# A two-branch transformer block on one core: where three tiles are transposed, who issues three small loads, and the order of two kinds of DMA transposes

## The chip, the cores and the metric

The kernel runs on one core of one Trainium2 chip. The time of a run is the device time in microseconds (us) of that core, from one launch; the figures below are medians of several runs. The engines named are TensorE (PE; its weight loads are PEld), VectorE (DVE), ScalarE (ACT), GpSimd (POOL) and SyncE (SP). SyncE computes nothing here: it issues DMAs, and ScalarE issues a few more.

## The reference

Input x has 2048 rows of 448 values in bf16. With xn = layernorm(x), the result is x + A(xn) + B(xn).

```python
# A: linear attention with 16 heads of 28
qkv = xn @ wqkv                                   # q, k, v
pq, pk = q @ w_phi[h], k @ w_phi[h]               # per head
phi_q = [softmax(pq), softmax(-pq)]               # the same for phi_k
kv, z = phi_k^T v, sum(phi_k)
A = (phi_q kv / (phi_q z + 1e-6)) @ wo
# B: on xn, with a normalization of its own
h  = gelu(layernorm(xn) @ w1)                     # (2048, 448)
x1 = xn + shift(h) @ w2                           # four column groups moved by 1, -1, 2, -2 rows
B  = x1 + gelu(layernorm(x1) @ w3) @ w4           # 448 -> 1792 -> 448
```

## The kernel before, in words

The 2048 rows are 16 tiles of 128. A small class, Recorder, takes every operation in the order in which the program states it (`op`, and its helpers `mm`, `tr`, `act`, `ew`, `dma`, `dma_t`), works out from the bytes that each reads and writes which semaphore waits are needed (`solve`, line 75), and then plays each engine's operations in that order. So each engine, and each queue of DMAs, runs strictly in program order; the order in the text is the schedule. In the profile all matmuls have line 188 (`mm`), PE transposes 192 (`tr`), ScalarE's operations 196 (`act`), those of VectorE and POOL 200 (`ew`), DMA transposes 203 (`dma_t`) and other DMAs 206 (`dma`).

**Loads (lines 339 to 358).** SyncE and ScalarE issue the tiles of x, wv and w1. Then SyncE issues, in this order: the transposes of the weights of k (`load_wT(1, c)`, four DMA transposes into hi), w2, the four loads of phi's blocks into bd (the line after 353, after POOL has zeroed bd), and two of the four transposes of q's weights (`load_wT(0, c)`). ScalarE's table of gelu is loaded by `table` (line 374).

**Normalization.** `ln1_stats` (line 430) takes VectorE's statistics of a tile (`bn_stats`, `bn_aggr`) and lets POOL work out the scale (`ln1_scale`: an addition and a power of -1/2); `ln1_apply` (448) writes the normed tile xn, on VectorE or POOL; `ln1_again` works out the scale of the second normalization for four tiles at a time.

**Transposing xn.** Every product of xn needs xnT, the tile with its columns on the partitions. `xn_T(i, b)` (line 467) does it with four PE transposes into bank b and one eviction by ScalarE. `xn_Td(i)` (473) does it with one DMA transpose from SyncE. Tiles 0 to 11 take the first way, 12 to 15 the second.

**Octets.** `octet(g)` (line 710) computes V = xn wv and the input of h (xn w1) of the four tiles of group g. It handles two tiles after the other in full-height matmuls of V and of w1 (`full`), then the half-height remainders of those two (`tail`, two at a time), then the half-height parts of the next two tiles, whose full parts follow. So the first use of an octet's third and fourth tile is in the half-height matmuls. `v_pair` evicts V by ScalarE or VectorE (`evac` names who does the third and fourth tile), `w_pair` evicts through gelu on ScalarE into h_tok. PE transposes of later tiles are put between the matmuls of an octet.

**What follows the octets.** `h_T(i)` (line 554) transposes tile i of h by DMA, SyncE again; `w2_mul(i)` (598) multiplies tile i with w2 and needs h of tiles i - 1, i and i + 1 because of the shifts. `fold(t, m, b, eng)` (457) multiplies a block of wT with phi's blocks bd, giving the weights of pq and pk at once. After octet 3 ScalarE issues w3 (`load_rest`, line 796). Then come the softmax inputs of k and q, with `w2_tile(4, 6)` (825) early among them, and `kv_tile`.

**The plan (from line 876).** Nine stages, each with two or three groups of w3 matmuls and a list of steps, written out by hand. N is `num_tile` (the attention's numerator and denominator of a tile: PE, a chain on VectorE, a product on POOL into o_tok), O is `o_T` (the DMA transpose of that tile of o into oT), E is `eq_T` (two DMA transposes of a tile of phi_q into eqT, one of four slots, which N of the tile four later reads), Ff is `fin_full` (the product with w4 and wo, which reads oT), St the store of a tile. SyncE issues E, O, St and the transposes of the second normalization's output in the order in which the list has them.

Of the kernel before, what the change touches and what calls it, by code (L numbers as in the profile page):

```python
# [5 lines left out]
ACT = mybir.ActivationFunctionType  # L6
# [202 lines left out]
def bass_parallel_sum__linear_kernel_hedgehog__mixer_s_mlp__prompt_kernel(  # L209
# [3 lines left out]
    H, DH = A_w_phi.shape[0], A_w_phi.shape[1]  # L213
# [3 lines left out]
    CR = 112  # L217
# [7 lines left out]
    with es:  # L225
        R = Recorder(nc, es)
# [13 lines left out]
        def new(name, cols, dt=BF16):  # L240
            return view(region(name, cols * DTB[dt]), cols, dt)
# [9 lines left out]
        xtok = new("xtok", NT * D).rearrange("p (t d) -> p t d", t=NT)  # L251
# [18 lines left out]
        bd = new("bd", 512).rearrange("p (c h e) -> p c h e", c=NC, h=4)  # L270
# [17 lines left out]
        st = new("st", NT * 8, F32).rearrange("p (t c) -> p t c", t=NT)  # L288
        mv = new("mv", NT * 8, F32).rearrange("p (t c) -> p t c", t=NT)
# [28 lines left out]
        def tview(b, n=512, base=0):  # L318
            return b[:, :].bitcast(BF16)[:, base:base + n]

        dve, pool = "DVE", "POOL"
# [28 lines left out]
        for c in range(NC):  # L350
            load_wT(1, c)
        R.dma(w2[0:CR, :, :], B_w2.rearrange("(m p) d -> p m d", p=CR))
        R.ew("POOL", "memset", bd[0:CR, :, :, :], 0.0)
        for k in range(4):
            p = slice(DH * k, DH * k + DH)
            R.dma(bd[p, :, k, 0:DH], A_w_phi[k::4].rearrange("c e f -> e c f"))
        for c in range(2):
            load_wT(0, c)

# [21 lines left out]
        R.ew(pool, "memset", epss[:, :, 1], LN_EPS * LN_EPS / (1.0 + LN_EPS))  # L381
        R.ew(pool, "memset", hT[:, :, 0:PAD], 0.0)
        R.ew(pool, "memset", hT[:, :, S + PAD:HW], 0.0)
        busy = gT[:, 0, 0, 0:256]
        R.ew(dve, "memset", busy, 1.0)
        R.ew(dve, "memset", vp[:, :, DH + 1:HP], 0.0)
# [22 lines left out]
        def lap(a):  # L409
            return bass.AP(a.tensor, a.offset, [list(a.ap[0]), [192, 2], [1, 256]])  # L410

        def halves(a):
            return a.rearrange("p (b e) -> p b e", b=2)

        def ln_stats(stt, mvt, src, i):
            R.ew(dve, "bn_stats", stt[:, i, 0:6], src[:, i, 0:D])
            R.ew(dve, "bn_aggr", mvt[:, i, 0:2], stt[:, i, 0:6])
# [8 lines left out]
        def ln_apply(eng, dst, src, mvt, rst, i, k=0):  # L426
            m, op = (mvt[:, i, 0:1], ALU.subtract) if eng == dve else (rst[:, i, 1:2], ALU.add)
            R.ew(eng, "tensor_scalar", dst, src, m, rst[:, i, k:k + 1], op0=op, op1=ALU.mult)

        def ln1_stats(a, n, neg):  # L430
            for i in range(a, a + n):
                ln_stats(st, mv, xtok, i)
            ln1_scale(a, n, neg)

        def ln1_scale(a, n, neg):
            R.ew(pool, "tensor_tensor", mv[:, a:a + n, 2:4], mv[:, a:a + n, 1:2].to_broadcast([128, n, 2]), epss[:, 0:n, :],
                 op=ALU.add)
            R.ew(pool, "tensor_tensor", rs[:, a:a + n, 2:4], mv[:, a:a + n, 2:4], mhalf2[:, 0:n, :], op=ALU.pow)
            if neg:
                R.ew(pool, "tensor_scalar", rs[:, a:a + neg, 1], mv[:, a:a + neg, 0], -1.0, 0.0, op0=ALU.mult,  # L440
                     op1=ALU.add)

        def ln1_again(a, n):
            R.ew(dve, "scalar_tensor_tensor", rs[:, a:a + n, 0], rs[:, a:a + n, 3], (1.0 + LN_EPS) ** -0.5,
                 mv[:, a:a + n, 2], op0=ALU.mult, op1=ALU.mult)
            R.ew(dve, "tensor_tensor", rs[:, a:a + n, 4], rs[:, a:a + n, 0], rs[:, a:a + n, 2], op=ALU.mult)

        def ln1_apply(eng, i):
            ln_apply(eng, halves(xn[:, i, :]), lap(xtok[:, i, :]), mv, rs, i, 2)
# [3 lines left out]
        def spin(n, cols):  # L453
            for _ in range(n):
                R.mm(banks[3][:, 0:cols], busy[:, 0:128], busy[:, 0:cols], True, True)
# [11 lines left out]
        def xn_T(i, b):  # L467
            b = banks[b]
            for kc in range(KC):
                R.tr(tview(b)[:, 128 * kc:128 * kc + 128], xn[:, i, 128 * kc:128 * kc + 128], ident[:, :])  # L470
            R.act(xnT[:, :, 128 * i:128 * i + 128], tview(b).rearrange("p (c d) -> p c d", c=KC), ACT.Copy)

        def xn_Td(i):
            R.dma_t(xnT[:, :, 128 * i:128 * i + 128], xn[:, i, :])

        def full(o, first):
            out, lhs, rhs, k = o
            for kc in (0, 3, 2 - k):
                R.mm(out, lhs(kc, 0, 128), rhs(kc, 0, 128), first and kc == 0, not first and kc == 2 - k)
# [14 lines left out]
        def v_pair(i, b):  # L494
            def out(eng="ACT"):
                vd = vaug[:, i:i + 2, :].rearrange("p t (h e) -> p t h e", e=HP)[:, :, :, 0:DH]
                vs = two(b)[:, :, 0:D].rearrange("p t (h e) -> p t h e", e=DH)
                if eng == "ACT":
                    R.act(vd, vs, ACT.Copy)
                else:  # L500
                    R.ew(eng, "tensor_copy", vd, vs)
            return [tok(wv, i, b), tok(wv, i + 1, b + 1)], out
# [51 lines left out]
        def h_T(i):  # L554
            R.dma_t(hT[:, :, PAD + 128 * i:PAD + 128 * i + 128], h_tok[i])
# [139 lines left out]
        def ln1_two(i):  # L695
            ln_stats(st, mv, xtok, i)
            ln1_apply(dve, i - 1)
            ln_stats(st, mv, xtok, i + 1)
            ln1_scale(i, 2, 1)
            ln1_apply(pool, i)  # L700

        def ln1_some(a, n):
            for i in range(a, a + n):
                ln1_stats(i, 1, 0)
                if i:
                    ln1_apply(dve, i - 1)
                if i == 4:
                    ln1_again(0, 4)

        def octet(g, evac="ACT", first="ACT", late=None):  # L710
            i = 4 * g
            v, w = v_pair(i, 0), w_pair(i, 2)
            v2, w2 = v_pair(i + 2, 4), w_pair(i + 2, 6)
            if g == 0:
                spin(19, 256)
                xn_T(0, 4)
                spin(5, 128)
                xn_T(1, 5)
                full(v[0][0], True)
                full(v[0][1], True)  # L720
                xn_T(2, 6)
                full(w[0][0], True)
                xn_T(3, 7)
                full(w[0][1], True)
            else:
                full(v[0][0], True)
                full(w[0][0], True)
                if i + 2 < 12:
                    xn_T(i + 2, 4)
                    xn_T(i + 3, 5)  # L730
                full(v[0][1], True)
                full(w[0][1], True)
            for p in (v, w):
                for o in p[0]:
                    tail(o, False)
            for p in (v2, w2):
                for o in p[0]:
                    tail(o, True)
            v[1](first)
            w[1]((0,))  # L740
            for o in v2[0]:
                full(o, False)
            if i + 4 < 12:
                xn_T(i + 4, 0)
                xn_T(i + 5, 1)
            if late:
                late()
            w[1]((1,))
            v2[1](evac)
            for o in w2[0]:  # L750
                full(o, False)
            w2[1]()

        ln1_some(0, 8)
        ln_stats(st, mv, xtok, 8)
        ln1_apply(dve, 7)
        octet(0, "DVE")
        ln_stats(st, mv, xtok, 9)
        ln1_scale(8, 2, 1)
        ln1_apply(pool, 8)  # L760
        ln1_again(4, 4)
        ln1_two(10)
        for i in range(4):
            h_T(i)
        octet(1, "DVE")
        ln1_apply(dve, 11)
        ln1_again(8, 4)
        ln1_stats(12, 2, 0)
        ln1_stats(14, 2, 0)
        for i in range(12, 16):  # L770
            ln1_apply(dve, i)
        h_T(4)
        for i in range(12, 16):
            xn_Td(i)
        for c in range(2, NC):
            load_wT(0, c)
        for i in range(5, 8):
# [71 lines left out]
        N, O, E, St, Ff = num_tile, o_T, eq_T, store, fin_full  # L849
# [23 lines left out]
        def stats2(i):  # L873
# [7 lines left out]
                      ]),  # L881
            (0, 2, 4, 6, [(N, 1, 0), (E, 5), (O, 1), (Ff, 0), (W, 11, 3), (sc, 2), (N, 2, 0), (E, 6), (O, 2), (N, 3, 6), (E, 7), (O, 3),
                          (Ff, 1)]),
            (0, 2, 6, [(Ff, 2), (St, 0), (ga, 2), (W, 12, 2), (N, 4, 0), (E, 8), (O, 4), (N, 5, 6), (E, 9), (O, 5), (W, 13, 3), (Ff, 3),
                       (St, 1),]),
            (0, 2, 6, [(Ff, 4), (St, 2), (W, 14, 2), (W, 15, 3), (sc, 3), (N, 6, 0), (E, 10), (O, 6), (N, 7, 6), (E, 11), (O, 7),
                       (Ff, 5), (St, 3), (ga, 3)]),
            (0, 2, 6, [(Ff, 6), (St, 4), (N, 8, 0), (E, 12), (O, 8), (N, 9, 6), (E, 13), (O, 9), (Ff, 7), (St, 5),]),
            (0, 2, 6, [(Ff, 8), (St, 6), (N, 10, 0), (E, 14), (O, 10), (N, 11, 6), (E, 15), (O, 11), (Ff, 9), (St, 7)]),
            (0, 2, 6, [(Ff, 10), (St, 8), (N, 12, 0), (O, 12), (N, 13, 6), (O, 13), (Ff, 11), (St, 9)]),  # L890
            (0, 2, 6, [(N, 14, 0), (O, 14), (Ff, 12), (St, 10), (N, 15, 2), (O, 15), (Ff, 13), (St, 11)])]
# [53 lines left out]
```

## Time and profile before

| | us |
|---|---|
| median of 3 runs | 181.6 |
| lowest and highest | 181.51, 182.17 |
| the profiled execution | 181.43 |
| its span, first to last instruction | 179.7 |

The profile is of one execution. Its times are microseconds from the start of the span. A row of the timeline has start, duration, engine, line, operation, tiles written and read, shape and how many were merged; in brackets stands how long the engine was idle before and what ended that. Names of buffers are without their numbers: xnT is also the memory of o and oT, vaug of the attention's scratch, hi of the first tiles of h and of the transposed weights. A q behind an engine's name (SPq, ACTq) marks an issue of a DMA; "to landing" is the time from issue to the arrival of the last byte's signal.

### The profile page before, as it was taken

What the parts mean: (1) busy time and instruction counts of PE and PEld (TensorE: products, weight loads), DVE (VectorE), ACT (ScalarE), POOL (GpSimd) and SP (SyncE); (2) the same over time, 40 slices, a digit from 0 to 9 for tenths busy, and PEclk for the clock granted to TensorE, in tenths of its full rate; (3) what the DMA queues carried; (4) which work ended last, traced back from release to release, by engine and by line L of the source; (5) the groups of instructions that cost most, each with busy time, mean ns of one, the idle gap of its engine ahead of it and who ended that gap; (6) DMA issues with size and microseconds to landing.
All of it is one profiled execution on the core that took longest, in us unless ns stands there. A gap on an engine that the chain in (4) does not pass through costs nothing.

```text
span 179.7 us, 3181 instructions
## 1 busy us (share of the span) xinstructions
PE 175.9 (98%) x1218; PEld 90.5 (50%) x1218; DVE 117.6 (65%) x269; ACT 80.2 (45%) x99; POOL 94.6 (53%) x144
## 2 busy tenths in 40 slices
PE   7999999999999999999999999999999999999994
PEld 5554655454445444654554654553554544635564
DVE  5898679659999999584594296196282352655531
ACT  2378881798999639777105104103206006014000
POOL 7774582067999797002457526037835063151660
PEclk9999999999999999999999999999999999999999
DMA  5998555499465498473245545432554654120231
GB/s 166 338 218 134 102 87 104 89 341 223 89 90 106 98 277 172 91 160 60 58 88 89 89 101 104 110 62 58 113 112 99 82 138 96 43 59 28 55 106 51
DMA packets 59142, 21.04 MB, mean 117 GB/s; under 512 B 50744, under 2 KB 58616, under 8 KB 59128
## 3 DMA queue, kind: packets, MB, share of 16 engines
q1 hardware_dynamic: 55656, 16.56, 45.8%
q10 hardware_dynamic: 3472, 4.29, 8.0%
q8 instruction: 9, 0.15, 0.3%
q14 instruction: 5, 0.04, 0.1%
HBM read 7.08 MB, written 1.84 MB: 50 GB/s over the span
## 4 chain that ended last, share of the span: by engine, by line
PE 95%; DVE 3%; ACT 0%; issue 0%
PE bank L188 93%; PE bank L192 2%; DVE vaug L200 1%; DVE st L200 1%; DVE xn L200 1%; ACT xnT L196 0%; DVE mv L200 0%; DVE gT L200 0%
## 5 line engine op out<-in xcount | busy, mean ns | idle before, releaser
L196 ACT ACTIVATE phik<-bank 128x1024 bf16<-128x1024 f32 (+1 forms) x44 | 40.2, 991 | 68.1 <-PE bank L188 67.9
L188 PE MATMUL bank<-gT,w 128*128 128x512 bf16 (+1 forms) x224 | 46.1, 380 | 0.1
L188 PE MATMUL bank<-w,phik 128*128 128x448 bf16 (+2 forms) x238 | 45.2, 342 | 0.0
L200 DVE TENSOR_TENSOR vaug<-bank,vaug 128x464 f32<-128x464 f32 (+3 forms) x65 | 33.1, 514 | 17.4 <-PE bank L188 12.3
L200 POOL TENSOR_TENSOR xnT<-vaug 128x196 bf16<-128x196 f32 (+1 forms) x32 | 18.0, 585 | 49.2 <-DVE vaug L200 49.2
L188 PEld LDWEIGHTS bank<-w,phik 128*128 128x128 bf16 x238 | 22.6, 98 | 18.4 <-issue 0.2
L188 PEld LDWEIGHTS bank<-gT,w 128*128 128x128 bf16 (+1 forms) x224 | 17.9, 97 | 24.0 <-issue 5.1
L200 POOL TENSOR_TENSOR phik<-phik,rks 128x896 bf16<-128x896 bf16 x15 | 25.8, 1754 | 1.0 <-DVE rks L200 0.9
L200 POOL TENSOR_TENSOR vaug<-xn,xtok 128x448 f32<-128x448 bf16 x16 | 16.3, 1029 | 1.4 <-DVE vaug L200 1.4
L200 DVE TENSOR_TENSOR xn<-bank,xn 128x448 bf16<-128x448 f32 x16 | 9.4, 597 | 11.5 <-PE bank L188 11.5
L200 DVE TENSOR_REDUCE ksum<-phik 128x32 f32<-128x896 bf16 x16 | 16.6, 1035 | 0.0
L200 DVE RECIPROCAL vaug<-bank 128x16 f32<-128x16 f32 x16 | 3.6, 228 | 17.9 <-PE bank L188 17.9
L188 PE MATMUL bank<-wo,xnT 128*128 128x448 bf16 (+3 forms) x68 | 14.7, 344 | 0.0
L200 POOL TENSOR_TENSOR rs<-mv,mhalf 128x2 f32<-128x2 f32 (+1 forms) x16 | 13.8, 863 | 1.3
L188 PE MATMUL bank<-w,hT 112*128 112x448 bf16 x64 | 14.2, 352 | 0.0
L188 PE MATMUL bank<-wv,xnT 128*128 128x448 bf16 (+1 forms) x64 | 14.0, 354 | 0.1
L188 PE MATMUL bank<-w,xnT 128*128 128x448 bf16 (+1 forms) x64 | 13.9, 352 | 0.0
L188 PE MATMUL bank<-wpk,xnT 128*128 128x448 bf16 (+1 forms) x64 | 12.2, 354 | 0.0
L188 PE MATMUL bank<-wpq,xnT 128*128 128x448 bf16 (+1 forms) x64 | 12.1, 354 | 0.0
L196 ACT ACTIVATE eq<-bank 128x896 bf16<-128x896 f32 x12 | 10.0, 923 | 1.4 <-PE bank L188 1.4
L200 POOL TENSOR_SCALAR mv<-mv 128x4 f32<-128x4 f32 x4 | 0.8, 203 | 18.2 <-DVE mv L200 18.2
L200 DVE BATCH_NORM_STATS2 st<-xtok 128x6 f32<-128x448 bf16 x16 | 9.8, 612 | 0.8 <-DMA xtok<-in_A_x_dram 0.7
(66 smaller groups left out, 179.2 us busy)
## 6 DMA issues: line engine op xcount, KB each, us to landing
w<-in_B_w_dram ACTq DMA_DIRECT2D x2, 896.0 KB, 6.4
out_dram<-vaug SPq DMA_DIRECT2D x15, 112.0 KB, 1.9
w<-in_B_w_dram ACTq DMA_DIRECT2D x1, 1568.0 KB, 8.7
xtok<-in_A_x_dram SPq DMA_DIRECT2D x2, 448.0 KB, 6.8
wo<-in_A_wo_dram SPq DMA_DIRECT2D x2, 224.0 KB, 2.8
w<-in_B_w_dram SPq DMA_DIRECT2D x1, 392.0 KB, 4.4
hi<-eq SPq DMA_TRANSPOSE x24, 2.5
xtok<-in_A_x_dram SPq DMA_DIRECT2D x3, 112.0 KB, 3.0
```

The source lines that it names most:

```text
L188: self.op("PE", lambda e: e.matmul(out, lhsT, rhs, start=start, stop=stop, skip_group_check=True), [out], [lhsT, rhs])
L192: self.op("PE", lambda e: e.transpose(out, in_, ident), [out], [in_, ident])
L196: self.op("ACT", lambda e: e.activation(out, in_, func, **kw), [out], [in_] + aps)
L200: self.op(eng, lambda e: getattr(e, name)(out, *args, **kw), [out], aps)
```

## The change

There are five edits.

1. Loads: zeroing bd and the four loads of phi's blocks move behind the zeroing of hT's edges, and so behind all the loads above on SyncE; three of the four are issued by ScalarE, behind its table load, one by SyncE.
2. Normalization: the statistics of tiles 8 to 13 are taken one tile at a time instead of in pairs (`ln1_two` is no longer used), and VectorE applies all of them; POOL applied tiles 8 and 10.
3. Transposing xn: PE does tiles 0 to 8; tiles 9, 10 and 11 go to SyncE as DMA transposes. Tiles 9 and 10 stand behind h_T(0) and h_T(1), tile 11 behind them, then h_T(2) and h_T(3); h_T(4) moves from ahead of tiles 12 to 15 to behind them.
4. V of tiles 6 and 7 is evicted by ScalarE (octet 1 without "DVE"; tiles 4 and 5 were ScalarE's before).
5. Plan: in the stages with N 4 and 5 and with N 8 and 9, O comes ahead of E.

```diff
@@ loads
-        R.ew("POOL", "memset", bd[0:CR, :, :, :], 0.0)
-        for k in range(4):
-            p = slice(DH * k, DH * k + DH)
-            R.dma(bd[p, :, k, 0:DH], A_w_phi[k::4].rearrange("c e f -> e c f"))
         for c in range(2):
             load_wT(0, c)
...
         R.ew(pool, "memset", hT[:, :, S + PAD:HW], 0.0)
+        R.ew("POOL", "memset", bd[0:CR, :, :, :], 0.0)
+        for k in range(4):
+            p = slice(DH * k, DH * k + DH)
+            R.dma(bd[p, :, k, 0:DH], A_w_phi[k::4].rearrange("c e f -> e c f"), "ACT" if k else "SP")
@@ octet
-                if i + 2 < 12:
-                    xn_T(i + 2, 4)
-                    xn_T(i + 3, 5)
+                if g == 1:
+                    xn_T(6, 4)
+                    xn_T(7, 5)
...
-            if i + 4 < 12:
-                xn_T(i + 4, 0)
-                xn_T(i + 5, 1)
+            for k in range(2 - g):
+                xn_T(i + 4 + k, k)
@@ octets and what stands between them
-        ln1_some(0, 8)
-        ln_stats(st, mv, xtok, 8)
-        ln1_apply(dve, 7)
+        ln1_some(0, 9)
         octet(0, "DVE")
-        ln_stats(st, mv, xtok, 9)
-        ln1_scale(8, 2, 1)
-        ln1_apply(pool, 8)
+        ln1_stats(9, 1, 0)
+        ln1_apply(dve, 8)
         ln1_again(4, 4)
-        ln1_two(10)
-        for i in range(4):
+        for i in range(10, 12):
+            ln1_stats(i, 1, 0)
+            ln1_apply(dve, i - 1)
+        for i in range(2):
             h_T(i)
-        octet(1, "DVE")
+        for i in range(9, 11):
+            xn_Td(i)
+        octet(1)
+        ln1_stats(12, 1, 0)
         ln1_apply(dve, 11)
+        xn_Td(11)
+        for i in range(2, 4):
+            h_T(i)
         ln1_again(8, 4)
-        ln1_stats(12, 2, 0)
+        ln1_stats(13, 1, 0)
+        ln1_apply(dve, 12)
         ln1_stats(14, 2, 0)
-        for i in range(12, 16):
+        for i in range(13, 16):
             ln1_apply(dve, i)
-        h_T(4)
         for i in range(12, 16):
             xn_Td(i)
+        h_T(4)
         for c in range(2, NC):
             load_wT(0, c)
@@ plan, two stages
-            ... (N, 4, 0), (E, 8), (O, 4), (N, 5, 6), (E, 9), (O, 5), ...
+            ... (N, 4, 0), (O, 4), (E, 8), (N, 5, 6), (O, 5), (E, 9), ...
-            ... (N, 8, 0), (E, 12), (O, 8), (N, 9, 6), (E, 13), (O, 9), ...
+            ... (N, 8, 0), (O, 8), (E, 12), (N, 9, 6), (O, 9), (E, 13), ...
```

More of the change, by code (lines that the diff above doesn't have):

```diff
@@ L883, in bass_parallel_sum__linear_kernel_hedgehog__mixer_s_mlp__prompt_kernel @@
                           (Ff, 1)]),
-            (0, 2, 6, [(Ff, 2), (St, 0), (ga, 2), (W, 12, 2), (N, 4, 0), (E, 8), (O, 4), (N, 5, 6), (E, 9), (O, 5), (W, 13, 3), (Ff, 3),
+            (0, 2, 6, [(Ff, 2), (St, 0), (ga, 2), (W, 12, 2), (N, 4, 0), (O, 4), (E, 8), (N, 5, 6), (O, 5), (E, 9), (W, 13, 3), (Ff, 3),
                        (St, 1),]),
@@ L887, in bass_parallel_sum__linear_kernel_hedgehog__mixer_s_mlp__prompt_kernel @@
                        (Ff, 5), (St, 3), (ga, 3)]),
-            (0, 2, 6, [(Ff, 6), (St, 4), (N, 8, 0), (E, 12), (O, 8), (N, 9, 6), (E, 13), (O, 9), (Ff, 7), (St, 5),]),
+            (0, 2, 6, [(Ff, 6), (St, 4), (N, 8, 0), (O, 8), (E, 12), (N, 9, 6), (O, 9), (E, 13), (Ff, 7), (St, 5),]),
             (0, 2, 6, [(Ff, 8), (St, 6), (N, 10, 0), (E, 14), (O, 10), (N, 11, 6), (E, 15), (O, 11), (Ff, 9), (St, 7)]),
```

## The prediction

> **What bounds the kernel now.** First I read busy time per engine and the chain that ended last, both on the page:
>
> ```profile
> PE 175.9 (98%) x1218; PEld 90.5 (50%) x1218; DVE 117.6 (65%) x269; ACT 80.2 (45%) x99; POOL 94.6 (53%) x144
> PE 95%; DVE 3%; ACT 0%; issue 0%
> ```
>
> TensorE holds 98% of the span and 95% of the chain. Matmul ends are modelled, so I then read starts in the timeline of PE through octets 1 and 2, where the change works:
>
> ```profile
> 18.46 0.61 PE L192 MATMUL bank<-ident,xn 128*128 128x128 bf16 x8
> 18.91 1.30 PE L188 MATMUL bank<-w,xnT 128*128 128x448 bf16 x6
> 20.05 0.73 PE L188 MATMUL bank<-wv,xnT 128*128 128x448 bf16 x3
> 21.18 0.61 PE L192 MATMUL bank<-ident,xn 128*128 128x128 bf16 x8
> 23.25 0.35 PE L188 MATMUL bank<-wv,xnT 64*128 64x448 bf16 x2
> ```
>
> Six 448-column matmuls start at 18.91 and the next group starts at 20.05: 0.19 us each, without a hole. So PE is fed here, and the kernel gains only by giving PE less to do, or by removing one of its few waits; a new wait of PE's is paid in full. The eight transposes at 18.46 (tiles 8 and 9) and at 21.18 (tiles 10 and 11) are what the change thins out; the row at 23.25 is the half-height matmuls of V for tiles 10 and 11, the first use of those two tiles.
>
> The second resource is SyncE's queue, which issues every DMA transpose in program order. Its timeline:
>
> ```profile
> 12.39 1.78 SPq L206 DMA_DIRECT2D bd<-in_A_w_phi_dram  x4
> 14.22 2.43 SPq L203 DMA_TRANSPOSE hi<-in_A_wqkv_dram  x2
> 16.69 1.74 SPq L203 DMA_TRANSPOSE hT<-hi  x1
> 18.48 1.26 SPq L203 DMA_TRANSPOSE hT<-hi  x1
> 19.79 1.27 SPq L203 DMA_TRANSPOSE hT<-hi  x1
> ```
>
> The rows follow each other without a hole: this queue is full here, one transpose each 1.31 us (18.48 to 19.79), the first of hT stretched to 1.79 (16.69 to 18.48). How long after its issue a transpose lands is told by tile hT between 16 and 26:
>
> ```profile
> DMA to landing us min/median/max: 2.5/2.5/3.0
> ```
>
> **The change part by part.**
>
> *Twelve transposes leave PE.* Eight take 18.91 - 18.46 = 0.45 us, so 0.056 each; tiles 9, 10 and 11 are twelve: **-0.68 us**, all of it on the chain. ScalarE loses their three evictions, which is worth nothing by itself.
>
> *Three DMA transposes join SyncE's queue, and three phi loads leave it.* The four loads hold the queue from 12.39 to 14.22, 0.46 each; with three gone, and wT's transposes ahead of the fourth, h_T(0) issues at 16.69 - 1.37 = 15.32. Behind it stand h_T(1), tile 9, tile 10, tile 11. One of the first two will be stretched as h_T(0) is now (1.79), the others take 1.31: tile 9 issues at 18.42, tile 10 at 19.73, tile 11 at 21.04. Are they normed by then? VectorE and POOL say so:
>
> ```profile
> 13.63 1.08 DVE L200 CAST vaug<-bank 128x896 bf16<-128x896 f32 x1
> 14.63 0.61 DVE L200 BATCH_NORM_STATS2 st<-xtok 128x6 f32<-128x448 bf16 x1
> 15.28 0.18 DVE L200 BATCH_NORM_AGGREGATE mv<-st 128x2 f32<-128x6 f32 x1
> 16.86 0.41 DVE L200 TENSOR_SCALAR xn<-xtok,mv,rs 128x512 bf16<-128x512 bf16 x1 [0.36 <-POOL rs L200]
> 12.57 0.69 POOL L200 TENSOR_TENSOR rs<-mv,mhalf 128x2 f32<-128x2 f32 x1
> ```
>
> Statistics cost 14.63 to 15.46 = 0.83, the apply 0.41, and POOL's square root 0.69 runs beside the next tile's statistics. After the cast, with 0.4 for ln1_again, tile 9 is normed at about 17.5, tile 10 at 18.7, tile 11 at 20.0: about 1 us ahead of the queue each time. VectorE keeps that pace because the cast of V of tiles 6 and 7, as long as the one at 13.63, moves to ScalarE, which gives up three evictions of tiles for it; banks 4 and 5, which that V leaves free, are wanted again only at 22.5. So the queue decides, not the engines.
>
> Landing 2.5 later: tile 9 at 20.92, tile 10 at 22.23, tile 11 at 23.54. PE, with its transposes gone, wants tile 9 at 21.18 - 0.23 = 20.95 (just met), and tiles 10 and 11 at 23.25 - 0.68 = 22.57. Tile 10 is there; **tile 11 is 0.97 late**, with 0.05 to start about **+1.0 us** of PE wait. No view shows this wait before, so I bound it: without the stretch 0.5; with the slowest landing of the row (3.0) 1.5. It can't be below zero, since PE waits or doesn't. I take 1.0, the median landing.
>
> At this place a page speaks against the stretch: the Trainium skill (Runtime: NRT & Kernel Launch, Instruction fetch mechanics) holds that refilling an engine's instructions is one queue bump, mostly hidden. This case has such a refill beside the stretched issue, by the DMA view from 16.3 to 16.6:
>
> ```profile
> q8 instruction: 1, 0.02, 19.8%
> ```
>
> By the page the stretch would be no part of the sum, and the wait 0.5 in place of 1.0; by the row the refill sits in the very slice where the queue slows, so the trace leans the other way without proving it.
>
> *What else is moved past SyncE.* h_T(2), h_T(3) and h_T(4) go behind the new ones. h_T(3) lands near 26.2, h_T(4) (now after tiles 12 to 15) near 33; their readers on PE are later by a microsecond or more. Tile 15 would issue at 21.04 + 6 x 1.31 = 28.9, land at 31.4, and is wanted by the row below at 31.82 - 0.68 + 1.0 = 32.1:
>
> ```profile
> 31.82 0.35 PE L188 MATMUL bank<-wv,xnT 64*128 64x448 bf16 x2
> ```
>
> All of this costs nothing in the forecast. From there the queue runs about 2 us later than now, which is the first rival below.
>
> *Three phi loads on ScalarE* stand between its table load and its first eviction:
>
> ```profile
> 3.27 1.28 ACT L372 ACT_TABLE_LOAD   x1 [3.27 <-issue]
> 6.10 0.60 ACT L196 ACTIVATE xnT<-bank 128x512 bf16<-128x512 bf16 x1 [1.55 <-PE bank L192]
> 7.07 0.60 ACT L196 ACTIVATE xnT<-bank 128x512 bf16<-128x512 bf16 x1 [0.37 <-PE bank L192]
> 2.75 0.49 ACTq L206 DMA_DIRECT2D xtok<-in_A_x_dram  x1
> 3.18 2.08 SPq L206 DMA_DIRECT2D xtok<-in_A_x_dram  x3
> ```
>
> 3 x 0.46 from 4.55 ends at 5.93, inside the 1.55 of idle; another 0.37 of slack lies ahead of the second eviction. Cost 0.
>
> *o ahead of q* matters where PE waits for o. In the stage that treats tiles 8 and 9:
>
> ```profile
> 132.10 1.13 POOL L200 TENSOR_TENSOR xnT<-vaug 128x196 bf16<-128x196 f32 x2 [2.59 <-DVE vaug L200]
> 133.97 2.50 SPq L203 DMA_TRANSPOSE hi<-eq  x2
> 136.52 1.26 SPq L203 DMA_TRANSPOSE xnT<-xnT  x1
> xnT<-xnT SPq DMA_TRANSPOSE x1, 4.3
> 125.86 2.81 PE L188 MATMUL bank<-w,phik 128*128 128x448 bf16 x14
> 128.51 0.73 PE L188 MATMUL bank<-wo,xnT 128*128 128x448 bf16 x3
> 138.07 2.81 PE L188 MATMUL bank<-w,phik 128*128 128x448 bf16 x14
> 140.84 0.36 PE L188 MATMUL bank<-wo,xnT 128*128 128x448 bf16 x1
> ```
>
> o of tile 8 is ready at 133.23, yet issues at 136.52 behind q's two transposes and lands 4.3 later, at 140.8; wo's product starts 2.77 after its group's start where the stage before needed 2.65. With o first it issues at 133.97 and lands 2.5 to 4.3 later, by 138.3 at worst: **-0.12 us**. q, then 1.3 later, is read a stage on. In the other stage nobody waits for o: 0.
>
> **Sum:** -0.68 + 1.0 - 0.12 = +0.20 us, against the profiled execution's 181.43 (span 179.7 and 1.7 around it): 181.6. The median of the runs shown is 181.60, 0.17 above that execution, so on its scale 181.8. With the wait at 0.5 and 1.5, and o worth 0 at the upper end, 181.3 to 182.4.
>
> **The rivals.**
>
> *The transposes are in time* (181.60 - 0.80 = 180.8). SyncE would have to reach tile 11 a microsecond sooner. For it: PE's transposes are surely gone and the queue is 1.37 earlier. Against it: a step of 1.31 in every undisturbed pair of rows. A plain store is quicker:
>
> ```profile
> 161.20 0.58 SPq L206 DMA_DIRECT2D out_dram<-vaug  x1
> ```
>
> With steps near that 0.58, tile 11 would be bounded by its norm at 20.0, land at 22.5, and no wait would be left. The Trainium skill says as much (Advanced Engine Details and Errata, X-Bar Transpose (TRN2)): transpose DMAs are as fast as regular ones. The trace doesn't agree: 1.27 against 0.58 to issue.
>
> *h_T(5) falls behind w3* (slower: 183.4). SyncE's ten steps from tile 11 to h_T(5) are 13.1 us, so it issues at 34.1, or 34.8 with one more stretched issue; w3's loads go out from ScalarE at 34.78 now, 35.1 then:
>
> ```profile
> 34.20 1.27 SPq L203 DMA_TRANSPOSE hT<-hi  x1
> hT<-hi SPq DMA_TRANSPOSE x1, 5.6
> 34.78 0.96 ACTq L206 DMA_DIRECT2D w<-in_B_w_dram  x2
> 35.52 1.65 SPq L203 DMA_TRANSPOSE hT<-hi  x1
> hT<-hi SPq DMA_TRANSPOSE x1, 8.0
> 41.85 0.92 PE L188 MATMUL bank<-w,hT 112*128 112x448 bf16 x4
> ```
>
> The transpose issued 0.58 ahead of w3 lands at 39.8, the next, after it, at 43.5. The four matmuls at 41.85 (42.2 then) read h_T(5). Ahead of w3 it is in time; behind it, with everything 0.3 later than now, it lands at 43.8 and PE waits about 1.6. It decides at the moment that w3 goes out, and h_T(5) is 0.3 to 1.0 us ahead of that, which speaks against it.
>
> *ScalarE's loads are late* (182.4). If three issues take what SyncE's three x loads at 3.18 take (2.08), they end at 6.63: 0.53 late, 0.16 of it beyond the slack; issued against a still fuller queue perhaps 0.6. Against it: ScalarE's own load at 2.75, with more to describe than a phi block, took 0.49 with the x loads in flight.
>
> That the swap of o and q does nothing (the late landing was chance) only takes back 0.12.
>
> **How the numbers follow.** Forecast, tile 11 late: 0.60. In time: 0.20. h_T(5) behind w3: 0.12. ScalarE late: 0.08. Predicted 181.8. Range 180.8 to 182.9: down to the first rival, over the forecast's own 181.3 to 182.4 and ScalarE's case; h_T(5)'s is left out. Half a per cent, 0.9 us, is about what a measurement of this kernel can tell from no change: below 180.7 only the lower half of "in time" reaches (0.09), above 182.5 h_T(5)'s case, part of ScalarE's and the forecast's tail (0.18); the rest, 0.73, is no change.
>
> **What would show it.** In the profile after, PE's list of waits should name a DMA of xnT, at about 22.6 us, near 1 us long; the page should count 1206 matmuls. SyncE should issue tile 11 near 21.0. If PE has no wait there, the queue term is wrong and the time falls to 180.8. If h_T(5)'s issue stands after w3's and PE waits before its matmuls near 42, the second rival holds. The row of wo at 140.8 should start 2.65 after its group. A first eviction later than 6.1 would show the ScalarE case.

## The result and the profile after

| us | changed | before, run beside it |
|---|---|---|
| runs | 14 | 14 |
| median | 182.75 | 181.70 |
| lowest | 181.76 | 181.48 |
| highest | 188.71 | 182.35 |

The fourteen runs of the changed kernel fall into two groups with nothing between them: ten from 181.76 to 183.29, and four from 187.86 to 188.71. The ratio leaves the four out (they are another course of events, shown below, and not noise): 1.0032 with a 95% interval from 1.0017 to 1.0047, which on 181.70 is +0.58 us, from 0.31 to 0.85. The prediction was 181.8, that is +0.20, with a range of 180.8 to 182.9. Run again (a_same below), the same kernel gave nine short runs of twelve, ratio 1.0012 [0.9993, 1.0031], and three long ones (186.96 to 188.25). So the usual run is 0.2 to 0.6 us slower than before: a change of a few tenths, as forecast, though the first interval lies wholly above the +0.20. And in 7 of 26 runs something costs 5 to 6 us more.

**The short run.** The profile of an execution of 181.84 us (a_same, the changed kernel unaltered, span 180.1) answers the rows that the prediction gave of octets 1 and 2. First PE's timeline:

```profile
18.79 0.39 PE L192 MATMUL bank<-ident,xn 128*128 128x128 bf16 x4
19.02 1.30 PE L188 MATMUL bank<-w,xnT 128*128 128x448 bf16 x6
...
20.72 0.73 PE L188 MATMUL bank<-w,xnT 128*128 128x448 bf16 x3
21.91 0.74 PE L188 MATMUL bank<-wv,xnT 128*128 128x448 bf16 x3 [0.46 <-DMA xnT<-xn]
23.54 0.57 PE L188 MATMUL bank<-wv,xnT 64*128 64x448 bf16 x2
...
24.24 1.31 PE L188 MATMUL bank<-wv,xnT 128*128 128x448 bf16 x6
```

The eight transposes at 18.46 are four at 18.79, and the eight at 21.18 are gone. Three matmuls are 0.57 us, so after the group at 20.72 the next should start at 21.29; it starts at 21.91. PE lost 0.62 there, and the bracket names what it waited for: the DMA transpose of tile 9. The row at 23.54, two half-height matmuls, lasts 0.57 where the same row of a kernel without a wait has 0.35 (23.62, shown under c_pe9_late): 0.22 more, for tile 11. From the group at 20.72 to the next full-height group, at 24.24, it is 3.52 us; without a wait it is 2.66 (21.43 to 24.09 in c_pe9_late). So PE lost 0.86 in all. Then the SyncE rows and the landings of tiles 9, 10 and 11, the first in the view of tile 9, the second in those of both others:

```profile
15.19 3.29 SPq L203 DMA_TRANSPOSE hT<-hi  x2
18.52 3.91 SPq L203 DMA_TRANSPOSE xnT<-xn  x3
```

```profile
xnT<-xn SPq DMA_TRANSPOSE x1, 3.3
xnT<-xn SPq DMA_TRANSPOSE x1, 2.5
```

The queue did what the sum said: tiles 9, 10 and 11 issue from 18.52, one each 1.3 us. Tile 9 lands 3.3 later, not 2.5.

**The long run.** The profiled execution that came with the result is one of the four (188.56 us). Its page, engines and chain:

```profile
PE 177.2 (95%) x1206; PEld 89.7 (48%) x1206; DVE 118.2 (63%) x270; ACT 79.5 (43%) x97; POOL 94.4 (51%) x146
```

```profile
PE 77%; DMA 11%; DVE 7%; POOL 2%; issue 1%; ACTq 0%; ACT 0%
```

Twelve matmuls fewer, as written (1218 before). But DMA, which had no entry in the chain of before, now holds 11% of it (by the page's row of lines, 6 are the transposes into hT, 2 those into xnT, and 3 the first loads of x). Its list of waits (engine, tile, line, releaser: us in total, times, longest) tells which DMA, and PE's timeline where:

```profile
PE bank L188 <- DMA hT<-hi: 3.9, 1, 3.9
PE bank L188 <- DMA xnT<-xn: 1.0, 1, 1.0
```

```profile
47.81 1.31 PE L188 MATMUL bank<-w,hT 112*128 112x448 bf16 x3 [3.92 <-DMA hT<-hi]
```

The one forecast wait is there with its 1.0 us; beside it stands one of 3.9 that the forecast had given only a chance. The matmuls at 47.81 read h_T(5). Its issue, the issue of w3 on ScalarE, and its landing:

```profile
36.47 2.75 SPq L203 DMA_TRANSPOSE hT<-hi  x2
36.48 0.92 ACTq L206 DMA_DIRECT2D w<-in_B_w_dram  x2
```

```profile
hT<-hi SPq DMA_TRANSPOSE x1, 11.3
```

The two went out within 0.01 us of each other, and the transpose landed 11.3 later, at 47.8, the moment that PE goes on. The wait is only part of the price. The table of windows has length, busy us (and count) of PE, PEld, DVE, ACT and POOL, the granted clock, DMA share and GB/s:

```profile
43.60:47.70 4.10, 0.29 (x2) 0.00 (x0) 4.00 (x7) 2.06 (x3) 3.26 (x2) 0.97 1.17 216
47.80:51.10 3.30, 3.29 (x11) 1.17 (x11) 2.39 (x6) 0.00 (x0) 3.29 (x2) 0.54 0.89 174
51.10:54.00 2.90, 2.90 (x19) 1.25 (x20) 2.83 (x5) 2.50 (x4) 1.91 (x2) 1.00 0.45 92
```

In the first window PE does nothing; in the second it runs 11 matmuls where the third, shorter one, has 19: the clock was granted at 0.54 for 3.3 us after the wait, so 3.3 x 0.46 = 1.5 us of work lost. The Trainium skill (TensorE: Matmul & The Clock Gate, Part 1: The HAM clock gate) gives half speed as the state after an idle window of about 3.4 us; these rows agree (3.9 us of idle, then 0.54), and the experiment with h_T(1) moved has a wait of 1.6 us of PE after which the clock stays at 1.00. Set matmul by matmul against a_same, this execution is 6.7 us longer (186.8 against 180.1): 0.8 is lost before octet 2, where PE and VectorE wait for the first loads, 0.3 more at tiles 9 to 11, 4.1 at h_T(5) and 1.5 in the slow clock. The race for h_T(5) is 5.6 of the 6.7.

### The profile page after: what moved, and what is told of

Its sections match the earlier page's. It is cut to its first block, busy times and chain, and to the rows that moved or that the text cites. A ratio compares the mean times of both kernels' runs of the same rounds, so it can differ in the third digit from the quotient of the medians.

```text
span 186.8 us, 3161 instructions
## 1 busy us (share of the span) xinstructions
PE 177.2 (95%) x1206; PEld 89.7 (48%) x1206; DVE 118.2 (63%) x270; ACT 79.5 (43%) x97; POOL 94.4 (51%) x146
## 4 chain that ended last, share of the span: by engine, by line
PE 77%; DMA 11%; DVE 7%; POOL 2%; issue 1%; ACTq 0%; ACT 0%
PE bank L188 77%; DMA hT<-hi 6%; DMA xtok<-in_A_x_dram 3%; DVE st L200 2%; DMA xnT<-xn 2%; DVE vaug L200 2%; DVE xn L200 2%; POOL rs L200 2%; DVE mv L200 1%; POOL mv L200 1%; ACTq L206 0%; ACT wv L196 0%; DVE rs L200 0%; PE bank L192 0%
## 5 line engine op out<-in xcount | busy, mean ns | idle before, releaser
L200 DVE TENSOR_TENSOR xn<-bank,xn 128x448 bf16<-128x448 f32 x16 | 9.8, 610 | 16.8 <-PE bank L188 16.6
L188 PE MATMUL bank<-w,hT 112*128 112x448 bf16 x64 | 15.0, 362 | 3.9 <-DMA hT<-hi 3.9
L200 DVE TENSOR_REDUCE ksum<-phik 128x32 f32<-128x896 bf16 x16 | 16.6, 1036 | 0.0
L200 POOL TENSOR_TENSOR rs<-mv,mhalf 128x2 f32<-128x2 f32 (+1 forms) x19 | 15.0, 788 | 1.5
L188 PE MATMUL bank<-wpq,xnT 128*128 128x448 bf16 (+1 forms) x64 | 13.1, 372 | 0.0
L188 PEld LDWEIGHTS bank<-w,hT 112*128 112x128 bf16 x64 | 6.0, 99 | 9.5 <-DMA hT<-hi 4.4
```

Of the source, the lines that this page charges most:

```text
L188: self.op("PE", lambda e: e.matmul(out, lhsT, rhs, start=start, stop=stop, skip_group_check=True), [out], [lhsT, rhs])
L200: self.op(eng, lambda e: getattr(e, name)(out, *args, **kw), [out], aps)
```

## Experiments

Eleven experiments, in three series (the first with a_same, a_w3late, a_xfirst and b_bd; the second with c_first_late, c_sp_late, c_pe9_late and b_w3late; the third with the rest); each ratio is against the kernel before in the same series, and the range of times is that of all runs of the kernel named. For the kernel before these were 181.47 to 183.31, 181.53 to 182.71 and 181.49 to 183.09 (29 runs in each series): none of its 101 runs, with the 14 above, is a long one.

**Theories.** *Queue:* SyncE's step of 1.3 us makes tiles 9 to 11 late by about the time that PE gained, and nothing else matters for the short run. *Start:* the changed kernel's first matmuls come at 5.80 in place of 5.46, so the phi loads on ScalarE cost 0.3 us (a small form of the third rival). *Race:* the long runs are h_T(5) losing to w3 (the rival with 183.4), against something of the chip that could hit any kernel.

**a_same: the changed kernel again.** No edit.

> The changed kernel again, unaltered. In the profile seen so far PE waited 1.1 us for the DMA transpose of a tile of xn, 4.1 us for the transpose of h_T(5), and lost about 1 us more among the first matmuls. Queue theory (SyncE's order makes tiles 9 to 11 late, and h_T(5) races with w3): the tile wait, about 1 us, is in every execution, the wait for h_T(5) is there or wholly absent, so the times fall in two groups, about 182 and about 188 us. Rival (that execution was disturbed from outside): the tile wait is gone as well and the median is near 181.0.

Measured: 181.84 to 182.65 and three at 186.96 to 188.25; ratio 1.0012 [0.9993, 1.0031]. Its issues beside the race, and h_T(5)'s landing:

```profile
34.96 1.27 SPq L203 DMA_TRANSPOSE hT<-hi  x1
35.30 1.05 ACTq L206 DMA_DIRECT2D w<-in_B_w_dram  x2
hT<-hi SPq DMA_TRANSPOSE x1, 6.0
```

Here h_T(5) leads by 0.34, lands at 40.9 and nobody waits. So 0.34 us at the issue decides over 5 us at the end.

**a_w3late: w3's loads three steps later.** The rest of the change stays.

```diff
-        load_rest()
         w2_tile(3, 2)
...
         ks(0)
+        load_rest()
```

> The changed kernel with w3's two loads issued by ScalarE after the first four tiles of k, about 5 us later. Theory of the race: h_T(5) has landed before w3's packets start, PE never waits for it, no run is above 184 us, and the median is 182.0 with the tile wait and the start unchanged. Rival: the long runs come from elsewhere, and one run in four still takes about 188.

Measured: 181.82 to 183.06 in 12 runs, none long; ratio 1.0022 [1.0008, 1.0036]. The issues of h_T(5) to h_T(7) and of w3, h_T(5)'s landing, and the wait of PE's weight loads for tiles of xnT:

```profile
34.88 4.51 SPq L203 DMA_TRANSPOSE hT<-hi  x3
39.70 0.43 ACTq L206 DMA_DIRECT2D w<-in_B_w_dram  x1
hT<-hi SPq DMA_TRANSPOSE x1, 3.1
PEld bank L188 <- DMA xnT<-xn: 1.7, 2, 1.5
```

Issued at the same time as in a_same, h_T(5) lands 3.1 later instead of 6.0, because w3 is not there yet. PE's three matmuls for tile 9 start at 22.77 in this execution, 1.2 after the group ahead of them should have ended, and another 0.15 is lost for tile 11. The median was to be 182.0 and is 182.37. The race theory holds, and the short run's loss is still there, so it is another matter.

**a_xfirst: tiles 9 to 11 one place ahead in the queue.** h_T(1) goes behind tile 11; w3 stays.

```diff
-        for i in range(2):
-            h_T(i)
+        h_T(0)
...
-        for i in range(2, 4):
+        for i in range(1, 4):
             h_T(i)
```

> The changed kernel with h_T(1) moved behind tile 11, so the DMA transposes of tiles 9, 10 and 11 each issue one place (1.3 us) sooner; the queue is as long as before from h_T(2) on. Queue theory: the wait of PE for xnT falls from about 1.1 to under 0.3 us and the fast runs are 0.8 us shorter than the unaltered changed kernel's; the race of h_T(5) gets worse, since PE and with it w3 come sooner and h_T(5) does not. Rival (the landing is late because of an instruction refill, not because of the place in the queue): the wait stays near 1 us and so does the time.

Measured: 181.41, 184.34, 185.44, 186.83, 187.49 and 188.9, so only one run of six escaped and no ratio can be given. The lowest, 181.41, is under all 29 of before. The profile is of the 184.34 run; the two longest waits of PE's weight loads for DMAs in it, the issue of the transpose in the first of them with that of w3 and its landing, and the window behind that wait:

```profile
PEld bank L188 <- DMA hi<-in_A_wqkv_dram: 1.8, 1, 1.8
PEld bank L188 <- DMA xnT<-xn: 0.9, 1, 0.9
```

```profile
33.68 2.16 SPq L203 DMA_TRANSPOSE hi<-in_A_wqkv_dram  x1
35.39 0.93 ACTq L206 DMA_DIRECT2D w<-in_B_w_dram  x2
hi<-in_A_wqkv_dram SPq DMA_TRANSPOSE x1, 7.0
```

```profile
40.70:44.00 3.30, 3.26 (x28) 1.86 (x29) 2.62 (x5) 1.26 (x3) 1.75 (x3) 1.00 1.18 208
```

This time another transpose was caught by w3, that of a block of q's weights (hi). It went out 1.71 ahead of w3 and was still under way then; it landed 7.0 after its issue, where the same transpose took 3.3 to 4.3 in the other twelve traces. PE waited for it and for a tile of h. I had expected the wait for xnT to be under 0.3; PE lost 0.8 on tile 11 (none on tile 9), since the three transposes began at 17.91 here and not at 17.44 as in c_first_late below, behind an h_T(0) stretched to 2.14, and tile 11 landed 3.2 after its issue. So the place in the queue is not all that sets it in one execution. That the race would be lost more often came out. The window shows the clock behind this wait: 1.00.

**b_bd: the phi loads alone.** The kernel before, with the first edit of the change and nothing else.

```diff
-        R.ew("POOL", "memset", bd[0:CR, :, :, :], 0.0)
-        for k in range(4):
-            p = slice(DH * k, DH * k + DH)
-            R.dma(bd[p, :, k, 0:DH], A_w_phi[k::4].rearrange("c e f -> e c f"))
...
         R.ew(pool, "memset", hT[:, :, S + PAD:HW], 0.0)
+        R.ew("POOL", "memset", bd[0:CR, :, :, :], 0.0)
+        for k in range(4):
+            p = slice(DH * k, DH * k + DH)
+            R.dma(bd[p, :, k, 0:DH], A_w_phi[k::4].rearrange("c e f -> e c f"), "ACT" if k else "SP")
```

> The kernel before with only the phi loads moved (three to ScalarE, the zeroing of bd with them). Theory that they delay the first loads of x, wv and w1: DMAs of x, wv and w1 land 0.3 to 0.8 us later, PE waits at 7 to 10 us, and the time is 0.4 to 0.9 us longer. Theory of the prediction (no cost, and nothing in the kernel before needs SyncE sooner): within 0.2 us of the kernel before.

Measured: 181.49 to 181.99, ratio 0.9986 [0.9974, 0.9998]. The edit costs nothing, and the start theory falls. ScalarE's rows of the changed kernel (a_same) show why:

```profile
3.26 1.28 ACT L368 ACT_TABLE_LOAD   x1 [3.26 <-issue]
3.30 2.28 ACTq L206 DMA_DIRECT2D bd<-in_A_w_phi_dram  x3
```

The three issues take 2.28, as the third rival had it (2.08), but they begin at 3.30, beside the table load, and end at 5.58, before the first eviction, at 6.24, is due.

**c_sp_late: the phi loads back on SyncE.** a_w3late, with all four phi loads at their old place ahead of the first transposes of q's weights.

```diff
+        R.ew("POOL", "memset", bd[0:CR, :, :, :], 0.0)
+        for k in range(4):
+            p = slice(DH * k, DH * k + DH)
+            R.dma(bd[p, :, k, 0:DH], A_w_phi[k::4].rearrange("c e f -> e c f"))
         for c in range(2):
             load_wT(0, c)
...
-        R.ew("POOL", "memset", bd[0:CR, :, :, :], 0.0)
-        for k in range(4):
-            p = slice(DH * k, DH * k + DH)
-            R.dma(bd[p, :, k, 0:DH], A_w_phi[k::4].rearrange("c e f -> e c f"), "ACT" if k else "SP")
```

> The changed kernel with w3 late and the four phi loads back on SyncE at their old place, all four ahead of the second pair of weight transposes. Queue theory: SyncE reaches h_T(0) and so tiles 9 to 11 about 1.3 us later, PE's wait for them grows from 0.6 to 1.2 us to about 2 to 2.5, and the time is 1.0 to 1.4 us longer than with w3 late alone (183.5). Rival (the tiles are late because of the instruction refill near 17 us, wherever they stand): the wait and the time stay within 0.4 us.

Measured: 182.73 to 183.74, ratio 1.0085 [1.0066, 1.0104], 0.0063 above a_w3late's (each against its own series): 1.1 us. SyncE's row of tiles 9 to 11 in a_w3late, then the same row here and the wait of PE's weight loads for them:

```profile
19.17 3.89 SPq L203 DMA_TRANSPOSE xnT<-xn  x3
```

```profile
20.22 3.90 SPq L203 DMA_TRANSPOSE xnT<-xn  x3
PEld bank L188 <- DMA xnT<-xn: 2.8, 2, 1.9
```

The tiles issue from 20.22 in place of 19.17, 1.05 later, and the waits of PE's weight loads for them are 2.8 in place of a_w3late's 1.7. The queue theory holds: in front of these tiles a microsecond of SyncE costs about a microsecond of the run (1.1 for 1.05).

**c_first_late: tiles 9 to 11 one place ahead, w3 late.** The edits of a_xfirst and a_w3late together.

> Both earlier edits in the changed kernel: h_T(1) behind tile 11, and w3's loads after the first four tiles of k. With the race of h_T(5) gone, what is left is the place of tiles 9 to 11 in the queue. Queue theory: PE's wait for xnT is 0.6 us as with the first edit alone, less than the 0.6 to 1.2 of the unaltered order; no wait for hT or for the weights of q; no run above 184; median 181.5, some 0.3 per cent below the kernel before (its best run alone was 181.41). Rival (the first edit's long runs did not come from w3): runs of 184 to 188 remain.

Measured: 181.29 to 183.0 in 12 runs, none long; ratio 0.9998 [0.9978, 1.0018]. In the profile (181.5) the only wait of PE for a DMA of xnT is this one:

```profile
31.48 0.35 PE L188 MATMUL bank<-wv,xnT 64*128 64x448 bf16 x1
32.02 0.35 PE L188 MATMUL bank<-wv,xnT 64*128 64x448 bf16 x1 [0.20 <-DMA xnT<-xn]
```

It is for tile 15, and by the starts PE lost 0.5 there; tiles 9 to 11 are in time. So one place earlier in the queue removes the wait for them, and the next late one is tile 15, further back in the same queue. The forecast of 0.6 us of wait for tiles 9 to 11 and of a median of 181.5 missed: no wait for them, 0.5 for tile 15, and a median of 181.89.

**c_pe9_late: tile 9 back on PE, w3 late.** Two transposes join SyncE instead of three.

```diff
-            for k in range(2 - g):
+            for k in range(2 if g < 2 else 0):
                 xn_T(i + 4 + k, k)
...
-        for i in range(9, 11):
-            xn_Td(i)
+        xn_Td(10)
```

> The changed kernel with w3 late and tile 9 back on PE, so that only tiles 10 and 11 go through SyncE, one place sooner each. PE does four transposes more (0.22 us). Queue theory: the wait was for tile 9, and tiles 10 and 11 are wanted 1.5 us later than it, so PE's wait is under 0.3 us, and the time is 181.4 (before, less 8 transposes 0.45, and less o's 0.12). Rival (whichever tile comes first through the queue is late, because the refill holds up all of them): PE waits 0.5 us or more for tile 10, and the time is 182.0 or above.

Measured: 181.06 to 182.22, ratio 0.998 [0.9966, 0.9995]. PE's timeline has no hole there:

```profile
21.43 0.73 PE L188 MATMUL bank<-w,xnT 128*128 128x448 bf16 x3
23.62 0.35 PE L188 MATMUL bank<-wv,xnT 64*128 64x448 bf16 x2
...
24.09 0.74 PE L188 MATMUL bank<-wv,xnT 128*128 128x448 bf16 x3
```

**c_pe9_late2: c_pe9_late once more, in the third series.** No further edit.

> Tile 9 back on PE and w3 late, again, to stand beside the two kernels of this call: 181.3, 0.2 per cent below the kernel before, no run above 184 us, no wait of PE for xnT.

Measured: 181.04 to 182.97, ratio 1.0002 [0.9979, 1.0026]. The median was to be 181.3 and is 181.99: the gain of the first time did not come again. What both series share is the lowest run, 181.06 and 181.04, against 181.53 and 181.49 for the kernel before: 0.45 lower, which is eight transposes of 0.056. So the matmuls saved are there when all goes well, and the spread of the runs (1.9 us against 1.6 before) eats the rest. A faster kernel isn't shown.

**c_pe9: tile 9 back on PE, w3 at its old place.**

> The changed kernel with tile 9 back on PE and w3 where the change has it, at the end of octet 3. SyncE's queue is one transpose shorter ahead of h_T(5), so h_T(5) issues 1.3 us sooner and PE, with the tile wait gone, about 0.8 us sooner. Theory of the race: h_T(5) then stands about 0.8 us ahead of w3 in place of 0.0 to 0.3, lands by 41 us, and no run is above 184; the median is 181.4. Rival (h_T(5) needs more room than that): some runs of 187 to 188 remain.

Measured: 181.07 to 182.67 in 12 runs, none long; ratio 1.0008 [0.9988, 1.0027]. The issues of h_T(5) and h_T(6) and of w3, the landing of the second of those transposes, and a wait of PE's weight loads:

```profile
34.50 2.58 SPq L203 DMA_TRANSPOSE hT<-hi  x2
35.63 0.95 ACTq L206 DMA_DIRECT2D w<-in_B_w_dram  x2
```

```profile
hT<-hi SPq DMA_TRANSPOSE x1, 11.0
PEld bank L188 <- DMA xnT<-xn: 0.9, 1, 0.9
```

One transpose fewer in the queue puts h_T(5) 1.13 ahead of w3, and it lands in 2.5. The next, h_T(6), goes out 0.2 behind w3 and takes 11.0, but it lands at 46.8 and isn't wanted before 49.2. In this profile w3 still catches a transpose, but one with time to spare. Two parts of the forecast missed: the tile wait was to be gone, yet in this execution tile 11 landed 3.2 after its issue (2.6 in c_pe9_late) and PE lost 0.9 for it; and the median is 181.88, not 181.4.

**b_w3late: w3 late in the kernel before.** A control for the others with that edit.

```diff
-        load_rest()
         w2_tile(3, 2)
...
         ks(0)
+        load_rest()
```

> The kernel before with w3 late, as a control. Before, h_T(6) and h_T(7) land late behind w3 too, but PE needs them only at 46 and 50 us. Both theories: within 0.2 us of the kernel before; if it is faster by more, w3's place is worth something of its own, and the comparisons with w3 late have to be read against this run.

Measured: 181.56 to 182.77, ratio 1.0003 [0.999, 1.0017]: the place of w3 is worth nothing by itself. Its first transposes, below those of the kernel before in the execution shown:

```profile
5.46 0.61 PE L192 MATMUL bank<-ident,xn 128*128 128x128 bf16 x4
5.79 0.57 PE L192 MATMUL bank<-ident,xn 128*128 128x128 bf16 x4 [0.29 <-DVE xn L200]
```

This kernel has none of the change's five edits, and starts at 5.79. So the 0.34 us between 5.46 and 5.80 in a_same need none of the change's edits; all twelve other traces start between 5.66 and 5.85.

**c_pe9_late_eo: q ahead of o again.** c_pe9_late with the old order in both stages.

```diff
-            ... (N, 4, 0), (O, 4), (E, 8), (N, 5, 6), (O, 5), (E, 9), ...
+            ... (N, 4, 0), (E, 8), (O, 4), (N, 5, 6), (E, 9), (O, 5), ...
-            ... (N, 8, 0), (O, 8), (E, 12), (N, 9, 6), (O, 9), (E, 13), ...
+            ... (N, 8, 0), (E, 12), (O, 8), (N, 9, 6), (E, 13), (O, 9), ...
```

> Tile 9 back on PE, w3 late, and q ahead of o again in both stages. Prediction's price of the swap: in the stage of tiles 8 and 9 the product of wo starts 0.1 to 0.25 us later after its group than the 2.65 with o first, and the median is 0.1 to 0.2 us above that of the run beside it. Rival: the late landing was chance, the start stays at 2.65 and the times are equal.

Measured: 181.06 to 182.5, ratio 0.9987 [0.9967, 1.0007], against 0.998 with the swap in one series and 1.0002 in the other. Its rows, in the stage that treats tiles 8 and 9:

```profile
136.91 1.26 SPq L203 DMA_TRANSPOSE xnT<-xnT  x1
...
138.46 2.81 PE L188 MATMUL bank<-w,phik 128*128 128x448 bf16 x14
141.11 0.73 PE L188 MATMUL bank<-wo,xnT 128*128 128x448 bf16 x3
```

o's transpose stands behind q's, yet wo starts 2.65 after its group, without a wait: o lands 2.5 after 136.91, in time. In this kernel the swap is worth nothing.

## Why the prediction was right or wrong

**Twelve transposes leave PE, -0.68.** Right. 1206 matmuls, and the lowest runs of the variants without a wait lie under before's by the price of their transposes (0.45 for eight).

**Tile 11 is late, +1.0.** Right in cause, in tile and nearly in size. The issues came 0.1 us behind the working (18.52 for 18.42), so the step of 1.31 and the one stretched issue held; and the norm was 1.1 us ahead of the queue, as worked out (tile 9's ends at 17.41 in a_same). For each trace one can work out when PE would want tile 11 without any wait (2.19 us after its last group of tile 8 starts, by 21.43 to 23.62 in c_pe9_late), when tile 11 lands, and what PE lost in octet 2 in all:

| us | tile 11 wanted | landed | late | PE lost |
|---|---|---|---|---|
| a_same | 22.9 | 23.7 | 0.8 | 0.9 |
| long run | 23.8 | 24.9 | 1.1 | 1.2 |
| a_w3late | 23.2 | 24.5 | 1.3 | 1.3 |
| c_sp_late | 23.0 | 25.3 | 2.4 | 2.4 |
| a_xfirst | 23.0 | 23.8 | 0.8 | 0.8 |
| c_pe9 | 23.2 | 24.0 | 0.8 | 0.9 |
| c_pe9_late | 23.6 | 23.2 | - | 0 |

To within the rounding, the loss is the lateness of tile 11 plus the 0.05 of the prediction, each time; in c_pe9_late2, c_pe9_late_eo and c_first_late, as in c_pe9_late, tile 11 lands before it is wanted and nothing is lost. For the changed kernel (the first three rows) that is inside the 0.5 to 1.5 given. What the prediction had wrong is where the loss shows: tile 9, called just met, landed 3.3 after its issue and not the 2.5 of the median row, so PE paid 0.62 of a_same's loss, and nearly all of the long run's and of a_w3late's, already there. That took nothing beyond what tile 11 would have cost. c_sp_late, c_first_late and c_pe9_late each moved the queue in one direction and PE's wait went with it, so that the queue is the cause is shown.

Why tile 9 takes 3.3 isn't shown, but it isn't the tile: a small fetch of instructions (queue q14) stands in the DMA view while that transpose is under way, and in all ten kept traces of the changed kernel and its variants the transpose issued 1.0 to 2.1 us ahead of the first of these fetches (20.4 to 21.6 us) lands 3.1 to 3.6 after its issue. It is tile 9 in three of them, tile 10 in six and h_T(1) in one. No run takes the fetch away.

**The rule on refills.** The prediction set a rule of the Trainium skill (Runtime: NRT & Kernel Launch, Instruction fetch mechanics), by which a refill is mostly hidden, against a stretched issue beside one. In a_same the queue runs 1.5 us earlier (h_T(0) at 15.19 for 16.69), yet the refill stands at nearly the same time, in the DMA view from 16.0 to 16.6, and it is again the transpose issued then, now h_T(1), that is stretched (the refill's row, then SyncE's):

```profile
q8 instruction: 1, 0.02, 13.5%
16.45 2.03 SPq L203 DMA_TRANSPOSE hT<-hi  x1
```

2.03 for 1.27. A second refill, between 31.5 and 34.8, shows the same: in all thirteen kept traces (before, the long run, and one of each experiment) the transpose issued within 0.4 us of it takes 1.69 to 2.43 to issue. So the stretch goes with the refill and not with the tile. No run takes a refill away, so this is an association and not yet a cause; but the term that the prediction kept in its sum was there. The sentence of the Trainium skill is about the engine whose instructions are fetched; what these rows show falls on the DMA queue of another.

**Transposes slower than stores.** The first rival (180.8, in time) fell: three transposes took 3.91 us to issue, 1.3 each and not 0.58. As far as the issue goes, that also speaks against the sentence of the Trainium skill beside it (Advanced Engine Details and Errata, X-Bar Transpose (TRN2)).

**o ahead of q, -0.12.** The number came out; whether it is the swap that earns it is not shown. SyncE's and PE's rows of a_same in that stage:

```profile
134.48 1.19 SPq L203 DMA_TRANSPOSE xnT<-xnT  x1
...
138.59 2.81 PE L188 MATMUL bank<-w,phik 128*128 128x448 bf16 x14
141.24 0.73 PE L188 MATMUL bank<-wo,xnT 128*128 128x448 bf16 x3
```

wo starts 2.65 after its group, as forecast. But c_pe9_late_eo has 2.65 with q first as well. o's late landing goes with a refill of instructions. The DMA view of before, from 138.4 to 138.6, in the time of that transpose, has this row:

```profile
q8 instruction: 1, 0.02, 34.7%
```

b_bd and b_w3late, with as many matmuls as before, landed it 4.4 and 4.3 after the issue. In all thirteen kept traces the transpose issued 1.2 to 2.2 us ahead of this refill lands 4.0 to 4.7 after its issue. In those three kernels the refill comes 0.35 to 0.64 us after the group starts and catches o; in the ten with eight or twelve transposes fewer on PE it comes 1.9 to 3.3 after it and catches another transpose. In c_pe9_late_eo it comes at 141.7, and o lands in 2.5. So once PE has fewer instructions the late landing is gone with either order, and the 0.12 comes without the swap. No run has the swap alone: in the kernel before, o first would have landed ahead of the refill, by the rows that the prediction gave, so there it may still be worth its 0.12.

**ScalarE's three loads, 0.** Right (b_bd), though not by the working: the three take 2.28 and not 1.4, and fit since they start beside the table load.

**The sum.** -0.68 + 0.86 - 0.12 is +0.06 for a_same, whose span is 0.40 longer than before's; the start of that execution, 0.34 later, is the rest. With the 1.3 that a_w3late lost in octet 2 the same sum is +0.5, so the size of the wait, which differs between executions, is one part of the spread. Over all short runs it is +0.58 [0.31, 0.85] in one series and +0.22 [-0.13, 0.56] in the other, where +0.20 was forecast.

**h_T(5) behind w3, 183.4 at 0.12.** (The second rival; where the prediction calls the later queue "the first rival below", it means this one.) The mechanism and the place were right; two sizes were wrong. The price was worked out as 1.6 us, from a transpose that before was issued behind w3 and landed 8.0 later; issued with w3 it took 11.3, and the idle gap then cost another 1.5 us of clock. The chance was taken from a lead of 0.3 to 1.0 us of h_T(5). The lead in two profiles was 0.34 and 0.01, and 7 of 26 runs lost it. The range left this case out. The median of all fourteen runs, 182.75, lies in it because only four of them were long: the ten short ones alone have 182.28, and that no more of them lost the race is luck. Against the theory that the chip does this to any kernel: none of 66 runs of five changed kernels with w3 late is long, nor any of the twelve of c_pe9, while 5 of 6 are in a_xfirst.

## What to carry to other kernels

Work moved from a full engine to a full queue is paid where its results are first read, so set each landing against its first reader. The whole loss is that of the piece that is latest against its reader (here tile 11); a piece that is "just met" by the median landing (here tile 9) may show part of it earlier. Where two queues issue without an order between them, a big load and small transposes with a deadline, the margin at the issue is to be set against how far the issues move from run to run; 0.3 us is none, and moving the big load behind the last of the small ones with a near deadline cost nothing here. When PE's idle gap grows to some microseconds (3.9 here; after 1.6 the clock stayed), add the slow clock after it to the price.

## What the runs showed of the hardware beyond that

A DMA transpose of SyncE that goes out together with the two loads of w3 from ScalarE, or behind the first of them, lands about when the second of them does: 11.3 us after its issue in the long run and 11.0 in c_pe9, where the second load takes 11.0 and 10.7. With a lead of 0.34 it lands with the first load, after 6.0 (a_same; that load takes 5.4). With a lead of 1.13, or with w3 late, it takes 2.5 and 3.1. A lead is enough only if the transpose is through by then: that of a_xfirst, which reads weights from memory and takes 3.3 to 4.3 elsewhere, went out 1.71 ahead and took 7.0.

ScalarE issues DMAs while its own table load runs (3.30 to 5.58 beside 3.26 to 4.54).

A refill of instructions goes with slower DMA transposes of SyncE, in all thirteen kept traces: 1.69 to 2.43 us to issue beside the one between 31.5 and 34.8 (1.27 undisturbed), 4.0 to 4.7 to land for the one under way when the refill at 138 to 148 comes (2.5 undisturbed). And the refill moves against the work: 0.35 to 0.64 us after the start of that group with 1218 matmuls, 1.9 to 3.3 with 1206 or 1210. That the deleted instructions move it fits, but these kernels differ in other edits too, and two executions of one kernel (c_pe9_late, c_pe9_late2) have 3.0 and 1.9.
